# When ScalarE's Exps run and which engine copies attention's tiles out of PSUM

## The chip, the cores and the metric

The kernel runs on one core of one Trainium2 chip. The metric is the device time in microseconds (us) of one execution, the median over several runs. Five engines work side by side, each on its own list of instructions in a fixed order: TensorE (PE in the profile; PEld are its weight loads), VectorE (DVE), ScalarE (ACT), GpSimd (POOL) and SyncE (SP), which here issues DMAs. TensorE writes to PSUM; VectorE and ScalarE read from it.

## The reference

Attention through 32 inducing points over 4 batches of 12480 tokens of 128 values, and behind it, on all 49920 rows, a feed-forward part of 2048 hidden values with a rational function between its two matrices:

```python
def mab(q, kv):
    s = scale * (q @ kv.transpose(0, 2, 1))
    s = s - s.max(-1, keepdims=True)
    a = np.exp(s)
    a /= a.sum(-1, keepdims=True) + 1e-09
    return a @ kv
h = mab(I, x)          # 32 inducing points attend to all tokens of the batch
x = mab(x, h)          # each token attends to the 32 results
...
h = x @ w_in
P = a[0] + a[1] * h + a[2] * h2 + a[3] * h3          # h2 = h*h, h3 = h2*h
Q = 1.0 + np.abs(b[0]) * np.abs(h) + np.abs(b[1]) * h2
return (P / (Q + 1e-06)) @ w_out
```

## The kernel before

**The feed-forward part** sets the beat. The hidden values lie across the 128 partitions, in 16 chunks. A block is 480 tokens, and a unit of work is one block and one pair `q` of chunks, a tile of 128x960: 4 batches x 26 blocks x 8 pairs are 832 units. `fast_ticks` (L777) writes out one tick for each unit, in which the stages of several units are interleaved: `first` makes `hp` in PSUM (TensorE, from the attention weights `at` and a table `st` of the batch), VectorE takes `u` from `hp` and makes a product `l`, GpSimd makes another `l` from `u`, ScalarE works on `u`, and `second` sums `po` from `l` and `w_out`. In even ticks VectorE has `u<-hp` and `l<-u,all,hp`, and GpSimd `l<-u,all`; in odd ticks VectorE has `l<-l,all,u` and `l<-hp,all,l`, and GpSimd `u<-l,all` and `l<-u`. Once in a block, `fetch` (L762) copies `po` to `oT` on VectorE, and SyncE stores it.

**ScalarE** computes the quotient through Ln and Sigmoid, which need different function tables. So it works in turns of eight ticks: four Lns on two units each (`u<-u`, 128x1920), a table load, four Sigmoids on the same (`u<-u,all`), a table load, and between them four Abs of later units (`u<-hp,all`). There are 104 turns. An Exp needs a table of its own; the Exps of attention stand at the place `turn == 4`, behind the Abs that follows the last Ln and ahead of the first Sigmoid, so that a turn with Exps has three table loads instead of two.

**Attention** runs beside it as Python generators that `side` (L680) moves on once in each tick. Each `yield` names what the next step costs on VectorE ("v"), TensorE ("pe") or GpSimd ("g"), and `side` takes it if the tick's share (`SPARE`) covers it; in one tick a generator takes steps of one kind only. Two generators run:

- `attend` works on the tokens of the batch at hand (`pass3`, L545): scores `pd` on TensorE, `amx` and `a` on VectorE, Exp of `a` on ScalarE, then `quotients` (L591): sums `asm` on VectorE, the scaling of `a` on GpSimd, transposes `pa` on TensorE, a rounded copy `hl[.,0]` of `pa` and, by VectorE, what the rounding left, `hl[.,1]`. `spread` sends `hl` to the tiles `at` by DMA.
- `ahead` (L633) prepares the next batch: `pass1` (L334) writes the scores of all tokens to `e`, seven groups of 480 columns; `exp_rows` (L380) takes their Exp in place, two groups at a time; `pooled` (L403) transposes `e` to `pt`, copies that to `eT` and sums `ph` with `x` on TensorE. Then come the tables `st` of the batch (`piece`, `linear`).

Two places of this have queues. An Exp is put in `exp_q` by `flush` (L395), and `run_act` (L224) issues all that is there at the next `turn == 4`. A copy on ScalarE goes through `act` (L214): it is put in `act_q`, issued a tick later, and its generator moves on after that. PSUM has one tile (`misc`) for all of attention's results; a generator holds it from the first matmul to `free`.

In what follows, `boot` is the time before the first unit, in which the first batch is prepared with nothing beside it. All engine calls pass through one helper, so that nearly all rows of the profile have its line, L157, and tiles are told apart by name.

Of the kernel before, what the change touches and what calls it, by code (L numbers as in the profile page):

```python
# [13 lines left out]
AF = mybir.ActivationFunctionType  # L14
# [3 lines left out]
P = 128  # L18
TP = 120
# [3 lines left out]
BT = HB * TP  # L23
# [149 lines left out]
class Kernel:  # L173
# [50 lines left out]
    def run_act(self, exps=True):  # L224
        while self.act_q and self.act_q[0][0] < self.tick:
            _, do, done = self.act_q.pop(0)
            do()
            done.append(1)
        if exps:
            for do in self.exp_q:  # L230
                do()
            self.exp_q = []

# [100 lines left out]
    def pass1(self, b):  # L334

        nc, ap = self.nc, self.ap
        X = mybir.AxisListType.X
        e = ap.tile([P, self.NG, BT], F32, tag="e", name=f"e{b}")
        mxs = ap.tile([P, self.NG, 2], F32, tag="mxs", name=f"mxs{b}")
        nc.gpsimd.memset(mxs, -3.0e38)  # L340
        xs = self.wide_columns(b) if self.boot else self.cols.pop((b, "a"))
        for g in range(self.NG):
            nb = min(4, self.NB - 4 * g)
            yield from self.landed("a", b, g)
            for j in range(nb):
                yield "pe", 0.8
                if j == 0:
                    pc = self.misc(f"pc{b}_{g}")
                nc.tensor.matmul(pc[:, 0:BT], self.ind[:, M * (3 - j):M * (7 - j)], next(xs), start=(j == 0), stop=(j == nb - 1))
            rows = slice(0, M * nb)  # L350
            for i in range(2):
                yield "v", 0.36
                c = slice(BT // 2 * i, BT // 2 * (i + 1))
                nc.vector.tensor_scalar(out=e[rows, g, c], in0=pc[rows, c], scalar1=1.0, scalar2=None, op0=ALU.mult, op1=ALU.max, accum_out=mxs[rows, g, i:i + 1])
            self.free()
        self.xs[b] = [self.x_rows(b, n) for n in range(4)]
        yield "v", 0.1
        mx = ap.tile([P, 1], F32, tag="mx", name=f"mx{b}")
        nc.vector.tensor_reduce(out=mx, in_=mxs.rearrange("p g i -> p (g i)"), axis=X, op=ALU.max)
        yield "pe", 0.2  # L360
        pm = self.misc(f"pm{b}")
        nc.tensor.transpose(out=pm[0:1, 0:P], in_=mx, identity=self.ident)
        yield "v", 0.3
        mt = ap.tile([1, 1, M], F32, tag="mt", name=f"mt{b}")
        nc.vector.tensor_reduce(out=mt[:, 0], in_=pm[0:1, 0:P].rearrange("o (j m) -> o m j", m=M), axis=X, op=ALU.max)
        self.free()
        nm = ap.tile([1, 4, M], F32, tag="H", name=f"nm{b}")
        nc.vector.tensor_scalar(out=nm, in0=mt.broadcast_to((1, 4, M)), scalar1=-1.0 / math.sqrt(C), scalar2=None, op0=ALU.mult)
        yield "pe", 0.2
        pb = self.misc(f"pb{b}")  # L370
        nc.tensor.matmul(pb[:, 0:4], nm.rearrange("o j m -> o (j m)"), self.ones, start=True, stop=True)
        yield "v", 0.1
        nmc = ap.tile([P, 1], F32, tag="nmc", name=f"nmc{b}")
        nc.vector.tensor_copy(out=nmc, in_=pb[:, 0:1])
        self.free()
        self.e[b] = e
        self.exps.append(lambda: self.exp_rows(b, e, nmc))
        self.flush()

    def exp_rows(self, b, e, nmc):  # L380

        g = self.e_done.get(b, 0)
        n = min(2, self.NG - g)
        rows = slice(0, M * min(4, self.NB - 4 * (g + n - 1)))
        if n == 2 and rows.stop < P:
            n, rows = 1, slice(0, P)
        self.nc.scalar.activation(e[rows, g:g + n], e[rows, g:g + n], AF.Exp, bias=nmc[rows], scale=1.0 / math.sqrt(C))
        self.e_done[b] = g + n
        if g + n < self.NG:
            if self.boot:  # L390
                self.exp_rows(b, e, nmc)
            else:
                self.exps.append(lambda: self.exp_rows(b, e, nmc))

    def flush(self):  # L395

        exps, self.exps = self.exps, []
        if self.direct:
            for do in exps:
                do()  # L400
        self.exp_q += [] if self.direct else exps

    def pooled(self, b, own=None):  # L403

        nc, ap = self.nc, self.ap
        e = self.e[b]
        acc = ap.tile([M, C + 1], F32, tag="acc", name=f"acc{b}")
        xs = self.xs.pop(b)

        def turned(g):  # L410
            rows = slice(0, M * min(4, self.NB - 4 * g))
            for c in range(HB):
                yield "pe", 0.22
                if c == 0:
                    pt = self.misc(f"pt{b}_{g}").rearrange("p (c n) -> p c n", c=HB)
                nc.tensor.transpose(out=pt[0:TP, c, rows], in_=e[rows, g, TP * c:TP * c + TP], identity=self.ident[rows, rows])
            eT = ap.tile([TP, HB, P], F32, tag="eT", name=f"eT{b}_{g}", bufs=2)
            yield from self.act(lambda: nc.scalar.activation(eT[:, :, rows], pt[0:TP, :, rows], AF.Identity, bias=0.0, scale=1.0))
            eTs.append(eT)

        eTs, early = [], int(self.boot)
        while self.e_done.get(b, 0) < self.NG:
            self.flush()
            yield "wait", 0
        if early:
            yield from turned(0)
        for g in range(self.NG):
            nb = min(4, self.NB - 4 * g)
            if g + early < self.NG:
                yield from turned(g + early)  # L430
            eT = eTs.pop(0)
            self.free()
            yield from self.landed("x", b, g)
            for k in range(HB * nb):
                j, c = divmod(k, HB)
                yield "pe", 0.2
                if k == 0:
                    ph = self.misc(f"ph{b}_{g}")
                if c == 0 and 0 < 4 * g + j < self.NB - 3:
                    xs.append(self.x_rows(b, 4 * g + j + 3))  # L440
                nc.tensor.matmul(ph[0:M, 0:C + 1], eT[:, c, M * j:M * j + M], xs[4 * g + j][:, c, :], start=(k == 0), stop=(k == HB * nb - 1))
            yield "v", 0.2
            if g == 0:
                nc.vector.tensor_copy(out=acc, in_=ph[0:M, 0:C + 1])
            else:
                nc.vector.tensor_tensor(out=acc, in0=ph[0:M, 0:C + 1], in1=acc, op=ALU.add)
            self.free()
        yield "v", 0.2
        rs = ap.tile([M, 1], F32, tag="rs", name=f"rs{b}")
        nc.vector.tensor_scalar(out=rs, in0=acc[:, C:], scalar1=1e-9, scalar2=None, op0=ALU.add)  # L450
        nc.vector.reciprocal(out=rs, in_=rs)
        yield "v", 0.2
        H = ap.tile([M, C], F32, tag="H", name=f"H{b}")
        nc.vector.tensor_scalar(out=H, in0=acc[:, 0:C], scalar1=rs, scalar2=None, op0=ALU.mult)
        yield "pe", 0.3
        pt = self.misc(f"HT{b}")
        nc.tensor.matmul(pt[:, 0:4 * M], H, self.ident4.rearrange("p a m -> p (a m)"), start=True, stop=True)
        yield "v", 0.2
        while own is None and self.scored < b - 2:
            yield "wait", 0  # L460
        HT = own if own is not None else ap.tile([C, 4 * M], F32, tag="HT", name=f"HT{b}", bufs=2)
        nc.vector.tensor_copy(out=HT, in_=pt[:, 0:4 * M])
        self.free()
        self.HT[b] = HT
# [80 lines left out]
    def pass3(self, b, groups):  # L545


        nc, ap = self.nc, self.ap
        X = mybir.AxisListType.X
        for fours in groups:  # L550
# [30 lines left out]

            if fours[-1] == self.NG - 1:
                self.scored = b
            self.exps.append(exps)
            self.flush()
            while not done:
                yield "wait", 0
# [3 lines left out]
    def quotients(self, b, r, nb, a):  # L591
        nc, ap = self.nc, self.ap
        rows = slice(0, M * nb)
# [10 lines left out]
        for c in range(HB):  # L604
            yield "pe", 0.25
            if c == 0:
                pt = self.misc(f"pa{b}_{r}")
            nc.tensor.transpose(out=pt[rows, TP * c:TP * c + TP], in_=a[:, c].rearrange("p j m -> p (j m)"), identity=self.ident[0:TP, 0:TP])
        hl = ap.tile([P, 2, BT], F32R, tag="hl", name=f"hl{b}_{r}", bufs=2)
        yield from self.act(lambda: nc.scalar.activation(hl[rows, 0], pt[rows, 0:BT], AF.Identity, bias=0.0, scale=1.0))  # L610
        yield "v", 0.65
        nc.vector.tensor_tensor(out=hl[rows, 1], in0=pt[rows, 0:BT], in1=hl[rows, 0].bitcast(F32), op=ALU.subtract)
        self.free()
# [335 lines left out]
```

## Time and profile before

| | before |
|---|---|
| runs | 2593.33, 2593.37, 2596.55 us; median 2593.37 us |
| profiled execution | 2594.75 us; its span 2592.9 us |
| granted TensorE clock, mean | 0.966 |
| busy share of the span | PE 87%, ACT 87%, DVE 85%, POOL 78% |
| instructions | PE 7508, DVE 2318, ACT 1590, POOL 1420 |
| table loads on ScalarE | 234, 300.2 us together |

The share of the span in which an engine is busy tells how full it is, and the chain that ended last tells whom the others wait for. In rows of the timeline the number in brackets is the engine's idle time ahead of the row, with the engine and tile that ended it.

### The profile page before, as it was taken

Reading aid. Unit: us, or ns where it says so; the run is one execution under the profiler, and the core shown is the slowest. Engines: PE = TensorE matmul, PEld = TensorE weight load, DVE = VectorE, ACT = ScalarE, POOL = GpSimd, SP = SyncE. Lnnn points to the kernel's source line nnn. Section 1 sums busy time; section 2 is a strip of 40 time slices with the busy share of each in tenths; the row PEclk is TensorE's granted clock in tenths of the full one; section 3 lists DMA queues with packets and bytes.
Section 4 is the critical chain, followed back from the end, with each engine's and each line's share of the span. In section 5 each row is a group of like instructions: output and inputs, shape, how many; then the busy total and the mean of one; then the engine's idle time right before and its main releaser. Section 6 shows DMA issues by size and latency. Waiting matters only on the chain.

```text
span 2592.9 us, 24006 instructions
## 1 busy us (share of the span) xinstructions
PE 2249.2 (87%) x7508; PEld 1233.8 (48%) x7508; DVE 2210.1 (85%) x2318; ACT 2244.9 (87%) x1590; POOL 2011.4 (78%) x1420
## 2 busy tenths in 40 slices
PE   7798888999899789989988898888888888888887
PEld 4544444555454355544544465444435434434333
DVE  6578778899899889899898888988889888888886
ACT  1488889989889999888899998899999999999996
POOL 2267767888787788888687887887888887888887
PEclk9699989999999999999999999999999999999999
DMA  7222201211222012112321131011101001000000
GB/s 251 73 62 78 73 27 52 71 50 31 70 83 80 19 31 76 50 48 63 92 55 48 35 88 38 16 42 31 46 27 50 27 20 38 20 22 24 17 17 17
DMA packets 117357, 133.68 MB, mean 52 GB/s; under 512 B 13544, under 2 KB 115816, under 8 KB 117224
## 3 DMA queue, kind: packets, MB, share of 16 engines
q1 hardware_dynamic: 117224, 132.06, 17.6%
q8 instruction: 64, 1.05, 0.2%
q14 instruction: 69, 0.57, 0.1%
HBM read 80.89 MB, written 25.56 MB: 41 GB/s over the span
## 4 chain that ended last, share of the span: by engine, by line
DVE 32%; PE 22%; ACT 19%; POOL 18%; issue 6%; DMA 1%; SPq 1%; DVEq 0%; POOLq 0%; ACTq 0%
DVE l L157 21%; ACT u L157 13%; POOL l L157 13%; PE po L157 13%; DVE u L157 7%; ACT L157 4%; POOL u L157 4%; PE hp L157 3%; PE ph L157 2%; PE pd L157 2%; DVE oT L157 1%; POOL a L157 1%; SPq L157 1%; DVE asm L157 1%; DMA x<-x_t 1%
## 5 line engine op out<-in xcount | busy, mean ns | idle before, releaser
L157 PE MATMUL po<-l,w_out 128*128 128x480 f32 x3328 | 1545.8, 592 | 188.4 <-POOL l L157 183.6
L157 PEld LDWEIGHTS po<-l,w_out 128*128 128x128 f32 x3328 | 607.3, 194 | 773.0 <-issue 419.7
L157 POOL TENSOR_TENSOR l<-u 128x960 f32<-128x960 f32 x416 | 932.2, 2241 | 34.7
L157 ACT ACTIVATE u<-u 128x1920 f32<-128x1920 f32 x416 | 739.8, 1799 | 193.2 <-DVE l L157 143.0
L157 PE MATMUL hp<-at,st 128*128 128x480 f32 x1664 | 742.7, 529 | 98.3 <-DVE l L157 91.1
L157 ACT ACTIVATE u<-u,all 128x1920 f32<-128x1920 f32 x416 | 766.1, 1887 | 1.2
L157 POOL TENSOR_SCALAR u<-l,all 128x960 f32<-128x960 f32 x416 | 445.5, 1071 | 392.8 <-DVE l L157 363.4
L157 DVE SCALAR_TENSOR_TENSOR l<-l,all,u 128x960 f32<-128x960 f32 x416 | 597.8, 1437 | 105.7 <-ACT u L157 105.3
L157 DVE SCALAR_TENSOR_TENSOR l<-hp,all,l 128x960 f32<-128x960 f32 x416 | 503.5, 1210 | 121.8 <-POOL l L157 114.0
L157 POOL TENSOR_SCALAR l<-u,all 128x960 f32<-128x960 f32 x416 | 555.6, 1336 | 64.7 <-DVE u L157 63.7
L157 DVE TENSOR_SCALAR u<-hp 128x960 int32<-128x960 int32 x416 | 477.0, 1147 | 75.6 <-PE hp L157 74.3
L157 PEld LDWEIGHTS hp<-at,st 128*128 128x128 f32 x1664 | 312.6, 193 | 431.3 <-issue 325.3
L157 DVE SCALAR_TENSOR_TENSOR l<-u,all,hp 128x960 f32<-128x960 f32 x416 | 500.3, 1203 | 0.3 <-ACT u L157 0.3
L157 ACT ACTIVATE u<-hp,all 128x960 f32<-128x960 f32 x416 | 434.7, 1045 | 36.4 <-PE hp L157 36.3
L157 ACT ACT_TABLE_LOAD x234 | 300.2, 1283 | 4.9 <-PEq L942 0.7
L157 PE MATMUL ph<-x,eT 120*32 120x129 f32 x832 | 105.8, 280 | 9.0 <-DMA x<-x_t 6.3
L157 PEld LDWEIGHTS pd<-HT,xTb 128*120 128x120 f32 x832 | 103.3, 198 | 9.7 <-DMA xTb<-x_c 4.3
L157 PE MATMUL pd<-HT,xTb 128*120 128x32 f32 x832 | 100.5, 277 | 5.2 <-DMA xTb<-x_c 4.1
L157 PEld LDWEIGHTS ph<-x,eT 120*32 120x32 f32 x832 | 88.9, 112 | 28.0 <-issue 21.5
L157 DVE COPY oT<-po 128x480 f32<-128x480 f32 x104 | 67.3, 647 | 21.6 <-PE po L157 21.3
L157 PE MATMUL po<-at,st 128*128 128x480 f32 x104 | 80.7, 776 | 0.0
L157 PE MATMUL pc<-xTa,ind 128*128 128x480 f32 x156 | 72.2, 566 | 1.9 <-DMA xTa<-x_c 1.9
(84 smaller groups left out, 621.6 us busy)
## 6 DMA issues: line engine op xcount, KB each, us to landing
x<-x_t SPq DMA_DIRECT2D x104, 240.0 KB, 3.5
xTb<-x_c SPq DMA_DIRECT2D x104, 240.0 KB, 2.8
at<-hl SPq DMA_DIRECT2D x416, 60.0 KB, 2.0
out<-oT SPq DMA_DIRECT2D x104, 240.0 KB, 2.0
xTa<-x_c SPq DMA_DIRECT2D x78, 240.0 KB, 2.8
xTw<-x_c SPq DMA_DIRECT2D x5, 960.0 KB, 10.3
raw<-w_in SPq DMA_DIRECT2D x4, 480.0 KB, 14.2
raw<-w_out SPq DMA_DIRECT2D x5, 384.0 KB, 5.9
```

The costliest lines, as they stand in the source:

```text
L157: ins = call(*args, **kw)
```

## The change

Two things are changed.

The Exps: each entry of `exp_q` now has a mark and the tick at which it came. The Exps of the tokens are marked `True` (soon), those of the batch ahead `False`. At `turn == 4` the queue is issued if an entry in it is marked soon or has waited 20 ticks; then all of it goes. And `exp_rows` takes up to three groups at a time (128x1440) instead of two (128x960).

The copies: outside `boot`, the copies `eT<-pt` and `hl<-pa` are VectorE's, as steps of kind "v" with a cost of 0.65, and don't go through `act` with its tick of delay.

```diff
@@ run_act
-        if exps:
-            for do in self.exp_q:
+        if exps and any(soon or self.tick - since >= 20 for do, soon, since in self.exp_q):
+            for do, _, _ in self.exp_q:
                 do()
             self.exp_q = []
@@ pass1
-        self.exps.append(lambda: self.exp_rows(b, e, nmc))
+        self.exps.append((lambda: self.exp_rows(b, e, nmc), False))
@@ exp_rows
-        n = min(2, self.NG - g)
+        n = min(3, self.NG - g)
         rows = slice(0, M * min(4, self.NB - 4 * (g + n - 1)))
-        if n == 2 and rows.stop < P:
-            n, rows = 1, slice(0, P)
+        if n > 1 and rows.stop < P:
+            n, rows = n - 1, slice(0, P)
...
-                self.exps.append(lambda: self.exp_rows(b, e, nmc))
+                self.exps.append((lambda: self.exp_rows(b, e, nmc), False))
@@ flush
-        self.exp_q += [] if self.direct else exps
+        self.exp_q += [] if self.direct else [(do, soon, self.tick) for do, soon in exps]
@@ pooled
-            yield from self.act(lambda: nc.scalar.activation(eT[:, :, rows], pt[0:TP, :, rows], AF.Identity, bias=0.0, scale=1.0))
+            if self.boot:
+                nc.scalar.activation(eT[:, :, rows], pt[0:TP, :, rows], AF.Identity, bias=0.0, scale=1.0)
+            else:
+                yield "v", 0.65
+                nc.vector.tensor_copy(out=eT[:, :, rows], in_=pt[0:TP, :, rows])
@@ pass3
-            self.exps.append(exps)
+            self.exps.append((exps, True))
@@ quotients
-        yield from self.act(lambda: nc.scalar.activation(hl[rows, 0], pt[rows, 0:BT], AF.Identity, bias=0.0, scale=1.0))
+        if self.boot:
+            nc.scalar.activation(hl[rows, 0], pt[rows, 0:BT], AF.Identity, bias=0.0, scale=1.0)
+        else:
+            yield "v", 0.65
+            self.cast(nc.vector, hl[rows, 0], pt[rows, 0:BT])
         yield "v", 0.65
         nc.vector.tensor_tensor(out=hl[rows, 1], in0=pt[rows, 0:BT], in1=hl[rows, 0].bitcast(F32), op=ALU.subtract)
```

Since a step of attention that is taken in another tick moves all that follow it, the order of the instructions changes in many places. Three of them, in rows of the built order (line, operation, result<-sources, shape; in `u_8_0` the numbers are block and pair, the last number only tells tiles apart).

ScalarE, in the first batch, around an Exp of the second batch's scores `e`; before, the first of four, which has a table switch to itself:

```order
L157 ACTIVATE u_9_0_1930<-hp_9_1_1927,all 128x960
L157 ACT_TABLE_LOAD
L157 ACTIVATE e_891<-e_891,nmc_1850 128x960
L157 ACT_TABLE_LOAD
L157 ACTIVATE u_8_0_1812<-u_8_0_1812,all 128x1920
```

and with the change, the second of three:

```order
L157 ACTIVATE u_12_0_2293<-hp_12_1_2290,all 128x960
L157 ACT_TABLE_LOAD
L157 ACTIVATE e_890<-e_890,nmc_1874 128x1440
L157 ACTIVATE a_5_2068<-a_5_2068 120x512
L157 ACTIVATE a_5_2068<-a_5_2068 120x4x64
L157 ACT_TABLE_LOAD
L157 ACTIVATE u_11_0_2184<-u_11_0_2184,all 128x1920
```

It is wider by half and stands with the Exps of the tokens, `a_5`, between one pair of table loads. The first of the three stands a turn earlier between two table loads of its own.

ScalarE, at the end of the Lns of block 5; before, a copy of the tokens' weights to `hl_2` stands behind the Abs of block 6:

```order
L157 ACTIVATE u_5_6_1487<-u_5_6_1487 128x1920
L157 ACTIVATE u_6_0_1514<-hp_6_1_1511,all 128x960
L157 ACTIVATE hl_2_1526<-pa_2_1521 128x480
L157 ACT_TABLE_LOAD
L157 ACTIVATE u_5_0_1396<-u_5_0_1396,all 128x1920
```

and with the change:

```order
L157 ACTIVATE u_5_4_1454<-u_5_4_1454 128x1920
L157 ACTIVATE u_5_6_1484<-u_5_6_1484 128x1920
L157 ACTIVATE u_6_0_1512<-hp_6_1_1509,all 128x960
L157 ACT_TABLE_LOAD
L157 ACTIVATE u_5_0_1389<-u_5_0_1389,all 128x1920
```

The copy is gone from this place between the last Ln and the first Sigmoid.

VectorE, around the rounding's rest `hl_5`; before, it stands in a tick whose number leaves 1 on division by 8 (the products of blocks 11 and 12 around it tell the tick):

```order
L157 TENSOR_SCALAR u_12_0_2309<-hp_12_0_2295 128x960
L157 SCALAR_TENSOR_TENSOR l_11_7_2311<-u_11_6_2280,all,hp_11_7_2277 128x960
L157 SCALAR_TENSOR_TENSOR l_10_6_2168<-l_10_6_2168,all,u_10_6_2164 128x960
L157 SCALAR_TENSOR_TENSOR l_12_0_2313<-hp_12_0_2295,all,l_12_0_2313 128x960
L157 TENSOR_TENSOR hl_5_2292<-pa_5_2287,hl_5_2292 128x480
```

and with the change:

```order
L157 TENSOR_SCALAR u_12_6_2375<-hp_12_6_2360 128x960
L157 SCALAR_TENSOR_TENSOR l_12_5_2377<-u_12_4_2346,all,hp_12_5_2343 128x960
L157 SCALAR_TENSOR_TENSOR l_11_4_2239<-l_11_4_2239,all,u_11_4_2235 128x960
L157 SCALAR_TENSOR_TENSOR l_12_6_2379<-hp_12_6_2360,all,l_12_6_2379 128x960
L157 TENSOR_SCALAR hl_5_2387<-pa_5_2382 128x480
L157 TENSOR_TENSOR hl_5_2387<-pa_5_2382,hl_5_2387 128x480
L157 TENSOR_SCALAR u_13_0_2407<-hp_13_0_2390 128x960
```

There the copy and the rest stand one behind the other on VectorE, six ticks later, in a tick that leaves 7.

More of the change, by code (lines that the diff above doesn't have):

```diff
@@ L398, in flush @@
         if self.direct:
-            for do in exps:
+            for do, _ in exps:
                 do()
-        self.exp_q += [] if self.direct else exps
+        self.exp_q += [] if self.direct else [(do, soon, self.tick) for do, soon in exps]
     def pooled(self, b, own=None):
```

## The prediction

> **What bounds the kernel now.** I read the engines' busy time first, then the chain of waits, and then one quiet turn row by row. A turn is eight ticks, that is one block of 480 tokens; I count it from the start of its first Sigmoid to that of the next turn. "Slot 3" means the ticks of `fast_ticks` whose number leaves 3 on division by 8.
>
> ```profile
> PE 2249.2 (87%) x7508; PEld 1233.8 (48%) x7508; DVE 2210.1 (85%) x2318; ACT 2244.9 (87%) x1590; POOL 2011.4 (78%) x1420
> DVE 32%; PE 22%; ACT 19%; POOL 18%; issue 6%; DMA 1%; SPq 1%; DVEq 0%; POOLq 0%; ACTq 0%
> ```
>
> Three engines stand within two points of each other and the chain spends its time on four of them, so none alone sets the pace. The chain of waits over one quiet turn near the end, where attention has nothing left to do, shows what does (start, us, engine and tile):
>
> ```profile
> 2457.12 1.90 ACT u L157
> 2459.05 0.38 DVE l L157
> ...
> 2461.48 0.57 DVE oT L157
> ...
> 2466.07 1.08 POOL u L157
> 2467.22 4.20 POOL l L157 x2
> 2471.45 1.22 DVE l L157
> ...
> 2473.73 1.13 DVE l L157
> 2474.95 2.75 ACT u L157 x2
> 2477.72 1.28 ACT L157
> 2479.01 1.90 ACT u L157
> ```
>
> It is a closed loop of 2479.01 − 2457.12 = 21.89 us: first Sigmoid, VectorE's products (with the copy `oT`), GpSimd's part of two pairs, VectorE again, the last Ln and the Abs behind it (2.75), a table load (1.28), the next Sigmoid. The timeline of the same turn shows the slack of those who wait (in brackets the idle time before a row, and who ended it):
>
> ```profile
> 2459.05 1.31 DVE L157 SCALAR_TENSOR_TENSOR l<-l,all,u 128x960 f32<-128x960 f32 x1 [0.67 <-ACT u L157]
> 2471.45 1.22 DVE L157 SCALAR_TENSOR_TENSOR l<-hp,all,l 128x960 f32<-128x960 f32 x1 [0.97 <-POOL l L157]
> 2476.87 1.22 DVE L157 SCALAR_TENSOR_TENSOR l<-hp,all,l 128x960 f32<-128x960 f32 x1 [0.89 <-POOL l L157]
> 2474.95 1.80 ACT L157 ACTIVATE u<-u 128x1920 f32<-128x1920 f32 x1 [1.22 <-DVE l L157]
> ```
>
> From this I take three rules. ScalarE waits 1.22 us before its last Ln, so a ScalarE copy anywhere between the first Sigmoid and that wait is free, while one between the last Ln and the Sigmoid (table load and Exp included) lies on the loop. An extra VectorE instruction is exposed in slots 3, 4 and 7, where VectorE works through from the Sigmoid to the pair that GpSimd needs (3, 4) or to the one that the last Ln needs (7). It is half covered in slots 5 and 6, where VectorE waits 0.97 for GpSimd, and covered in slots 0, 1 and 2, behind the last Ln's input, where 0.89 + 0.67 = 1.56 us of waits stand ready to take it.
>
> A later turn with attention's work in it bears this out.
>
> ```profile
> 1986.23 3.68 ACT L157 ACTIVATE u<-u,all 128x1920 f32<-128x1920 f32 x2
> 2005.34 1.80 ACT L157 ACTIVATE u<-u 128x1920 f32<-128x1920 f32 x1 [2.51 <-DVE l L157]
> ...
> 2009.41 1.06 ACT L157 ACTIVATE a<-a 120x1024 f32<-120x1024 f32 x1
> 2010.49 1.28 ACT L157 ACT_TABLE_LOAD   x1
> 2011.78 1.90 ACT L157 ACTIVATE u<-u,all 128x1920 f32<-128x1920 f32 x1
> ```
> ```profile
> 1991.64 0.66 DVE L157 COPY oT<-po 128x480 f32<-128x480 f32 x1 [0.84 <-PE po L157]
> 1992.22 0.68 DVE L157 TENSOR_REDUCE amx<-pd 120x16 f32<-120x512 f32 x1
> ...
> 1997.26 0.68 DVE L157 TENSOR_TENSOR a<-pd,amx 120x512 f32<-120x512 f32 x1
> ...
> 2005.17 0.68 DVE L157 TENSOR_REDUCE amx<-pd 120x16 f32<-120x512 f32 x1
> ...
> 2008.49 0.68 DVE L157 TENSOR_TENSOR a<-pd,amx 120x512 f32<-120x512 f32 x1
> ...
> 2013.71 1.22 DVE L157 SCALAR_TENSOR_TENSOR l<-l,all,u 128x960 f32<-128x960 f32 x1 [2.36 <-ACT u L157]
> ```
>
> It takes 2011.78 − 1986.23 = 25.55, or 3.66 over the quiet 21.89. Of that, 1.06 + 1.28 = 2.34 are the Exp and its second table load; the rest, 1.3, is what two VectorE rows in slots 3 and 5 (0.68 each) cost, for the wait before the last Ln grew from 1.22 to 2.51. The two rows in slots 0 and 1 (2005.17, 2008.49) cost nothing: VectorE still waits 2.36 for the Sigmoid. So exposed time counts at 1.29/1.36 = 0.95. And an earlier turn with two ScalarE copies off the loop:
>
> ```profile
> 927.14 0.58 ACT L157 ACTIVATE eT<-pt 120x512 f32<-120x512 f32 x1
> ...
> 936.11 0.56 ACT L157 ACTIVATE hl<-pa 128x480 fp32r<-128x480 f32 x1
> 938.57 1.80 ACT L157 ACTIVATE u<-u 128x1920 f32<-128x1920 f32 x1 [0.21 <-DVE l L157]
> 942.64 3.69 ACT L157 ACTIVATE u<-u,all 128x1920 f32<-128x1920 f32 x2
> ```
>
> The copies shrank the wait to 0.21 and the turn, begun at 920.82, took 21.82: no more than a quiet one. Most of what the change takes from ScalarE was free there.
>
> **The change part by part.** Durations, from the groups of instructions kept apart by shape (count | busy us, mean ns):
>
> ```profile
> L157 ACT ACT_TABLE_LOAD x234 | 300.2, 1283 | 4.9 <-PEq L942 0.7
> L157 ACT ACTIVATE e<-e,nmc 128x960 f32<-128x960 f32 x12 | 12.9, 1094 | 30.7 <-DVE nmc L157 30.6
> L157 ACT ACTIVATE e<-e,nmc 64x480 f32<-64x480 f32 x4 | 2.8, 692 | 0.0
> L157 ACT ACTIVATE eT<-pt 120x512 f32<-120x512 f32 x24 | 13.9, 583 | 19.6 <-PE pt L157 19.6
> L157 ACT ACTIVATE hl<-pa 128x480 fp32r<-128x480 f32 x24 | 13.4, 560 | 6.8 <-PE pa L157 4.6 <-PE po L157 1.1 <-PE hp L157 0.9
> L157 DVE COPY oT<-po 128x480 f32<-128x480 f32 x104 | 67.3, 647 | 21.6 <-PE po L157 21.3
> L157 DVE TENSOR_TENSOR hl<-pa,hl 128x480 fp32r<-128x480 f32 x24 | 15.6, 649 | 1.8 <-ACT hl L157 1.8
> L157 DVE TENSOR_REDUCE asm<-a 120x16 f32<-120x512 f32 x24 | 16.2, 675 | 0.8 <-ACT a L157 0.8
> ```
>
> *ScalarE's part of the loop (term 1).* In the built order the table loads fall from 234 to 230, and all four are second switches between the last Ln and the first Sigmoid: 4 × 1.283 = −5.1. The Exps of `e` outside the start go from nine of 128x960 and three of 64x480 to six of 128x1440 and the same three. No 1440 row exists; the line through 692 at 480 and 1094 at 960 gives 1496, so 9 × 1.094 − 6 × 1.496 = 0.9 less (bounds 0 and −0.9, since the work on the elements stays and only the fixed part can go). Of the 48 ScalarE copies that go (21 `eT`, 27 `hl`), four stand on the loop before (two of each), with one gate copy whose place shifts off it: about 5 × 0.57 = −2.9. The others ran under the 1.22 us wait and give nothing. Sum: −8.9.
>
> The Trainium skill ("ScalarE: Activation LUTs", section "What ACT_TABLE_LOAD costs") puts a switch at about 1283 ns of load and 1380 ns of drain. The load agrees with the row; the drain doesn't show, as the load at 2477.72 starts 0.02 behind the Abs and the Sigmoid follows it at once. By that page four switches would be worth 10.6 instead of 5.1.
>
> *VectorE (terms 2 and 3).* It gains those 48 instructions, each beside the 0.65 for a PSUM source of 480 columns (`oT`, `hl`) or 0.68 for 120x512 (`asm`'s row for its width); an `eT` of the last, half-filled group has fewer columns, about 0.41, scaled by width. In all 18 × 0.68 + 3 × 0.41 + 27 × 0.65 = +31. What of it counts hangs on the slots, and these move for all of attention's work, as the copies no longer wait for ScalarE and so shift what follows. I sorted all extras by slot from the built order, and priced them by the rows above and their like:
> - exposed (3, 4, 7): 87 → 123 instructions, 45.4 → 62.4 us (+17.0). Twelve `eT` and four `hl` copies come in, and the sums `asm` go from 8 to 17 and the gate scalings `gs` from 4 to 12, while the products `st` go from 8 to 3. Slot 7 alone gains 16.
> - half covered (5, 6): 75 → 92 instructions, 37.8 → 51.0 us, with 14 `hl` pairs in slot 6. Beyond 0.97 in each turn: 5.1 → 8.6 (+3.5).
> - covered (0, 1, 2): 132 → 127 instructions, 69.3 → 70.2 us. Beyond 1.56 plus the turn's Exp stretch it falls from 6.6 to 2.1; the straight lines below give this class no price, so I count nothing, and −4.5 as the bound.
>
> The price per exposed us I take as 1.0. A straight line through all turns of this trace, their length against the extras of each class, gave 0.9 to 1.3 for it, 0.1 to 0.5 for the half-covered, and about nothing for the covered ones. The lower bound is 0.5: before 1991.64 VectorE waits 0.84 for TensorE inside an exposed slot, and over the kernel 21.3 us go there ahead of `oT`, in which extras could vanish.
>
> *What else moves.* Nothing is queued behind a waiting Exp on ScalarE, as a closure held back issues nothing; what waits for it is `pooled` and then the next batch's tables, of which the built order still writes the last 512 columns in block 22 of 26 and the linear part in block 25, for use at the end of the block after next. On VectorE each new copy has the next pair's `u` behind it and waits itself for TensorE's transposes, issued at least a tick (2.7 us) earlier: 0. DMAs are the same in number. TensorE's attention matmuls bunch a little more (the most crowded turns have 8.4 us of them, from 7.8): 0, at worst +4. At the start the copies stay, and its Exps join: within 0.5 either way.
>
> **Sum:** −8.9 + 17.0 + 3.5 = +11.6 on the profiled execution's 2594.75 (span 2592.9 and 1.85 around it) gives 2606.4. The median of the runs is 1.4 below that execution, so I say **2605.0**. By the skill's page it would be +6.1. Ends: −8.9 − 4.5 + 0.5 × 17 = −5; −8.0 + 1.3 × 17 + 0.45 × 13.2 + 4 = +24.
>
> **The rivals.** (a) *All VectorE time is exposed.* If slots 5 and 6, filled with pairs, use up the wait for GpSimd and so delay the next pair, 31 of VectorE count: +22, 2615. For it: two copies in one tick make 1.3 us against 0.97. Against: the rows at 2005.17 and 2008.49. 0.11.
> (b) *Cancels.* Exposed extras fill TensorE's 21.3 us ahead of `oT` and count half: −8.9 + 8.5 + 1.8 = +1, 2595. 0.20.
> (c) *Faster.* VectorE's chain is not lengthened, since where the extra stands the wait for GpSimd or TensorE moves with it, and term 1 stays alone: −8.9, 2584.5. For it: every single VectorE wait quoted is of about the size of one copy. Against: 1.22 → 2.51 above. 0.20.
> (d) *ScalarE sets the pace.* Then all it sheds counts: 5.1 + 0.9 + 48 × 0.56 = 33, 2560. For it: 87%. Against: 1.22 us of idle time in every quiet turn, and 21.82 with two copies in it. 0.04. The Trainium skill ("Perfetto Trace Analysis", section "Identifying the Most-Contended Engine") would look at the fullest engine first, and that speaks for this one; the turn of 21.82 us speaks against it.
> That Exps don't join is none: the built order shows 26 → 22 Exp stretches.
>
> **How the numbers follow.** My forecast has 0.45, the rivals 0.11, 0.20, 0.20 and 0.04. A measurement of this kernel tells 0.2% (5 us) from no change. Slower: 0.45 + 0.11 = 0.56; same: 0.20; faster: 0.24. The likeliest case's own range is 2598 to 2611; 8 in 10 needs (b) and (c) and half of (a): 2584 to 2618. Left out are (d), the lower half of (c) and the upper of (a), some 0.2.
>
> **What would show it.** Right: 230 table loads; VectorE's busy time up by about 31, ScalarE's down by about 33; the wait for VectorE ahead of ScalarE's Lns (143.0 us in the row below) larger by 25 to 45, since ScalarE loses work inside that wait and the loop grows; quiet turns still 21.9; turns with slot-7 extras longer by their rows' length. Wrong: if turns with extras in slots 3, 4 and 7 stay at 21.9, or if `hl` pairs in slot 6 lengthen their turn by more than 1.3 − 0.97.
>
> ```profile
> L157 ACT ACTIVATE u<-u 128x1920 f32<-128x1920 f32 x416 | 739.8, 1799 | 193.2 <-DVE l L157 143.0 <-POOL l L157 46.9 <-POOL x L157 2.2
> ```

## The result: slower, and by more than twice what was forecast

| | before | with the change |
|---|---|---|
| median of the runs (lowest, highest) | 2593.35 us (2590.50, 2596.55) | 2621.82 us (2620.76, 2629.04) |
| ratio to before | | 1.0115 (95% interval 1.0094 to 1.0137) |
| span of the profiled execution | 2592.9 | 2619.3 |
| turns 0 to 101 together, over 21.9 us each | 189.1 | 221.4 |
| of it turns 0 to 5 | 28.5 | 35.2 |
| of it turns 22 to 29, 48 to 55 and 74 to 81 (around the switches to the next batch) | 36.8 | 65.0 |
| of it all others | 123.7 | 121.2 |

Forecast were +11.6 us and at most 2618; measured are +28.5. The lower part of the table is summed over the lengths of the turns, from first Sigmoid to first Sigmoid; the turns are counted from 0, and 26 of them make a batch. Outside the start of the kernel and the three switches of batches the change even wins 2.5 us. Where the time is lost doesn't yet tell why, since the change also moves work from one turn to another. (The time ahead of the first Sigmoid, 121.8 us before and 115.7 after, tells nothing: in two kernels of the runs below whose instructions are the same up to there, the probes in slots 5 and 1, it was 115.9 and 121.2.)

The page after, busy times and the engines' shares of the chain:

```profile
PE 2252.6 (86%) x7508; PEld 1229.1 (47%) x7508; DVE 2232.2 (85%) x2366; ACT 2217.3 (85%) x1534; POOL 2006.3 (77%) x1420
DVE 32%; PE 25%; ACT 17%; POOL 14%; issue 5%; DMA 2%; SPq 2%; DVEq 0%; ACTq 0%; POOLq 0%
```

ScalarE is 28 us less busy and VectorE 22 us more; in the chain TensorE (22% to 25%), the DMAs and SyncE's queue have grown. The groups of instructions by shape show the sizes of the change itself:

```profile
L157 ACT ACT_TABLE_LOAD x230 | 295.1, 1283 | 4.8 <-PEq L950 0.7
L157 ACT ACTIVATE e<-e,nmc 128x1440 f32<-128x1440 f32 x8 | 11.9, 1494 | 30.4 <-DVE nmc L157 30.3
L157 DVE TENSOR_SCALAR hl<-pa 128x480 fp32r<-128x480 f32 x23 | 14.9, 649 | 0.6 <-issue 0.4
L157 DVE COPY eT<-pt 120x512 f32<-120x512 f32 x18 | 12.3, 681 | 0.0
L157 DVE COPY eT<-pt 120x256 f32<-120x256 f32 x3 | 1.2, 413 | 0.0
```

All are as estimated, to 3 ns: 1494 for the wide Exp, 649 and 681 for the copies. The lines that no part of the prediction spoke of are among the waits (engine and tile, released by whom: us, times, longest), before and then after:

```profile
PEld pd L157 <- DMA xTb<-x_c: 4.3, 2, 2.5
PE pd L157 <- DMA xTb<-x_c: 4.1, 2, 2.4
```
```profile
PEld pd L157 <- DMA xTb<-x_c: 14.1, 8, 2.5
PE pd L157 <- DMA xTb<-x_c: 13.2, 8, 2.4
```

TensorE waits for the loads of the tokens' columns, three times as long. Three turns show where: number 23, 49 and 75, each the 24th of its batch, take 31.71, 32.04 and 31.81 us; before, these took 23.27, 22.15 and 21.89. The chain of waits through turn 75 (1950.14 to 1981.95):

```profile
1946.26 2.99 DMA xTb<-x_c
1949.25 0.04 issue
1949.29 1.02 PE pd L157 x8
...
1957.61 0.57 DVE oT L157
1958.19 0.02 issue
1958.20 0.34 SPq L157
1958.55 0.05 issue
1958.59 0.03 SPq L157
1958.62 0.03 issue
1958.65 2.91 DMA xTb<-x_c
1961.56 0.04 issue
1961.61 1.02 PE pd L157 x8
1962.63 5.00 PE po L157 x8
```

Two loads stand in the chain, and ahead of the second one SyncE: its store of `oT` had to wait for VectorE's copy, and the load was the next in the queue. What SyncE did there, in its own timeline:

```profile
1940.25 5.96 SPq L157 DMA_DIRECT2D at<-hl  x8
1946.26 2.02 SPq L157 DMA_DIRECT2D xTb<-x_c  x4
1958.20 0.34 SPq L157 DMA_DIRECT2D out<-oT  x1
1958.65 1.82 SPq L157 DMA_DIRECT2D xTb<-x_c  x4
```

Ahead of the first load stand eight small DMAs `at<-hl`, which keep SyncE's queue for 5.96 us.

### The profile page after: what moved, and what is told of

Same layout as the page of the kernel before. It is cut to its first block, busy times and chain, and to the rows that moved or that the text cites. A ratio compares the mean times of both kernels' runs of the same rounds, so it can differ in the third digit from the quotient of the medians.

```text
span 2619.3 us, 23913 instructions
## 1 busy us (share of the span) xinstructions
PE 2252.6 (86%) x7508; PEld 1229.1 (47%) x7508; DVE 2232.2 (85%) x2366; ACT 2217.3 (85%) x1534; POOL 2006.3 (77%) x1420
## 4 chain that ended last, share of the span: by engine, by line
DVE 32%; PE 25%; ACT 17%; POOL 14%; issue 5%; DMA 2%; SPq 2%; DVEq 0%; ACTq 0%; POOLq 0%
DVE l L157 20%; PE po L157 14%; ACT u L157 13%; POOL l L157 11%; DVE u L157 7%; ACT L157 4%; PE hp L157 4%; PE ph L157 3%; POOL u L157 3%; SPq L157 2%; PE pd L157 2%; DVE oT L157 1%; DVE asm L157 1%; DMA xTb<-x_c 1%; PE pc L157 1%
## 5 line engine op out<-in xcount | busy, mean ns | idle before, releaser
L157 DVE SCALAR_TENSOR_TENSOR l<-l,all,u 128x960 f32<-128x960 f32 x416 | 584.4, 1405 | 104.2 <-ACT u L157 104.2
L157 DVE SCALAR_TENSOR_TENSOR l<-hp,all,l 128x960 f32<-128x960 f32 x416 | 503.5, 1210 | 115.9 <-POOL l L157 106.9
L157 ACT ACT_TABLE_LOAD x230 | 295.1, 1283 | 4.8 <-PEq L950 0.7
```

Source lines behind the costliest of these rows:

```text
L157: ins = call(*args, **kw)
```

## The experiments

Theory A was that these late loads are what the prediction missed; B, that the copies cost VectorE more than I took; C, that the Exps' wait makes the next batch's preparation late, so that work piles up at the switch.

### Loads written out earlier

`columns` issues the load of a group's fourth block only when the first block of that group is asked for. The first kernel writes each load out right behind the last score matmul of the block whose buffer it takes:

```diff
@@ columns
                 if n + 4 < self.NB:
                     ts.append(self.x_columns(b, n + 4, kind))
+                if kind == "b":
+                    yield
@@ pass3
                     nc.tensor.matmul(pc[0:TP, M * j:M * j + M], xT[...], self.HT[b][:, 0:M], start=True, stop=True)
+                    if j % HB == HB - 1:
+                        next(self.cols[b, "b"])
```

> The changed kernel, but each load of the tokens' columns xTb is written out right behind the last score matmul of the block whose buffer it takes, instead of when the next block is asked for; nothing else is edited. Theory A (late loads: in turns 23, 49 and 75 TensorE waits twice for the load of a group's fourth block, which SyncE has only just issued; each such turn is 6.9 us longer than the VectorE slots and table loads account for, 20.8 together): the three turns fall from 31.8 to about 25, TensorE's wait for xTb from 13.2 to under 3, the time from 2621.8 to 2601 (to 2610 if TensorE's crowd of matmuls stays in the way). Theory B (the copies on VectorE cost more per us than I took) and theory C (the Exps' wait moves the next batch's tables to the batch's end, where two generators' work collides): within 5 us of 2621.8.

Measured: 2599.32 us, ratio to before 1.0026 (1.0015 to 1.0036); TensorE no longer waits for `xTb`, and turns 23, 49 and 75 take about 26.75 us each. 22.5 us came back, as A has it; B and C don't allow for that. The control on the kernel before:

> The kernel before with the earlier xTb loads alone, a control for the first run. TensorE waits 4.1 us for xTb before, so there is little to win; the order of attention's work moves a little (excess by slots and table loads 131.2 against 125.2): 2590 to 2600 by every theory. Much faster than 2590 would mean that the loads cost more than their waits show.

Measured: 2611.37 us, 1.0066 (1.0052 to 1.0080), slower and outside all expectations. The edit also moves attention's ticks, since `landed` now sees the loads: by the names of the tiles, 1981 of the 7508 places in TensorE's order hold another matmul than without the edit, against 134 in the changed kernel. Here other loads (`xTa`, 6.6 us of TensorE's waits from 1.9) became late as well, and the control doesn't tell what the edit itself is worth. So loads had to be made punctual without moving anything else; that is the third set of runs.

### Each part alone

The Exps' part with the copies left on ScalarE, and the copies' part with the Exps as before:

> Only the Exps' part of the change: the queue waits and takes three groups, the copies eT and hl stay on ScalarE with their delay. The next batch's HT then comes in block 22, 21 and 21 of the batch, against 18, 14 and 10 before and 20, 20 and 20 with the whole change. Theory A or B: table loads and slots give 127.9 us of excess over quiet turns, against 125.2 before, so 2593 to 2598. Theory C: 2605 to 2618, with long turns near the end of each batch.

> Only the copies' part of the change: eT and hl by VectorE without a delay, the Exps two groups at a time and at the next switch. VectorE's slots by the built order: exposed 54.3 us (before 45.4, whole change 62.4), half covered 60.6 (37.8, 51.0), covered 68.8. Excess over quiet turns by the prices of the prediction 134.4 us against 125.2: 2602. Theory B: 2612 or more. Theory C: 2602 or less, since the next batch's HT comes in blocks 18, 13 and 6, early.

Measured: 2653.77 us, 1.0241 (1.0227 to 1.0255), and 2644.87 us, 1.0206 (1.0192 to 1.0220). Both parts alone are slower than both together, which none of the theories had: the Exps' part lies above every expectation for it, the copies' part where only B (2612 or more) put it. The chain through turn 50 of the Exps' part (35.47 us long) shows SyncE's queue at its worst: from the store of `oT` on, the chain runs for over 10 us through it and sixteen DMAs `at<-hl`, and then a load lands and TensorE goes on:

```profile
1357.44 0.33 SPq L157
...
1358.48 0.54 SPq L157
...
1359.07 0.58 SPq L157
...
1367.52 0.59 SPq L157
...
1368.15 2.96 DMA xTb<-x_c
...
1371.15 1.81 PE pd L157 x8
```

Each small DMA takes SyncE about 0.59 us, so two tiles `at` (sixteen of them) ahead of a load delay it by some 10 us. Which loads are hit depends on where the ticks fall; that this is why the two parts' costs don't add is tested next.

### SyncE's queue alone

Here `at<-hl` and `out<-oT` are put in a list and written out a tick later, two in a tick, while loads are written out at once. Every instruction on TensorE, VectorE, ScalarE and GpSimd keeps its place, in all four kernels by the names of the tiles in their traces; only SyncE's order differs.

```diff
@@ spread
-                    self.nc.sync.dma_start(out=at[M * k:M * k + M, j].bitcast(F32), in_=hl[rows, k % 2].bitcast(F32))
+                    self.later_dma(1, at[M * k:M * k + M, j].bitcast(F32), hl[rows, k % 2].bitcast(F32), (b, 2 * r + h))
@@ fetch
-        self.nc.sync.dma_start(out=self.out[:, t:t + BT], in_=oT)
+        self.later_dma(1, self.out[:, t:t + BT], oT)
@@ side
         self.tick += 1
+        self.run_dma(2)
...
+    def run_dma(self, most):
+        while self.dma_q and most and self.dma_q[0][0] <= self.tick:
+            _, out, in_, _ = self.dma_q.pop(0)
+            self.nc.sync.dma_start(out=out, in_=in_)
+            most -= 1
```

The list is emptied ahead of a first use of `at` and of a new `hl`.

> The kernel before with SyncE's queue alone changed: the small DMAs of spread (at<-hl, eight for a tile) and the store out<-oT are held back by a tick and written out two in a tick, while loads go at once; on TensorE, VectorE and ScalarE every instruction stands in the order of before. Theory D (loads of attention that stand in SyncE's queue behind eight at<-hl at 0.6 us each, or behind a store that waits for oT, come late, and TensorE's fixed order turns that into a stall of everything): TensorE's waits for loads, 12 us before, fall by half or more, 2575 to 2588. Theory E (what the order costs beyond VectorE's slots is TensorE's own crowd of attention matmuls): 2590 to 2596, no change.

> The changed kernel with the same change of SyncE's queue alone; the order on TensorE, VectorE and ScalarE is the changed kernel's. Theory D: from 2621.8 to 2595 or less, since its 31 us beyond slots and table loads are mostly late loads, and what stays over the run above is the slots' share, 134.3 - 125.2 = 9 us. Theory E: 2615 to 2622.

> The Exps' part alone with the same change of SyncE's queue. Theory D: from 2653.8 to 2600 or less; over the kernel before with this queue about 3 us by slots and table loads (127.9 against 125.2). Theory E: above 2640.

> The copies' part alone with the same change of SyncE's queue. Theory D: from 2644.9 to 2605 or less; over the kernel before with this queue about 9 us by slots and table loads (134.4 against 125.2). Theory E: above 2630.

| | queue as it was | queue relieved | ratio to before as it was |
|---|---|---|---|
| before | 2593.0 | 2579.12 | 0.9960 (0.9946 to 0.9975) |
| whole change | 2621.82 | 2596.71 | 1.0017 (1.0007 to 1.0028) |
| Exps' part | 2653.77 | 2608.98 | 1.0057 (1.0041 to 1.0074) |
| copies' part | 2644.87 | 2599.68 | 1.0033 (1.0021 to 1.0045) |

All four fall, by 14, 25, 45 and 45 us, and TensorE's waits for `xTb` are gone, but for one of 1.3 us in the Exps' part. That the queue costs this much (D) is shown, and that TensorE's crowd alone accounts for the excess (E) falls. In size D holds for before and the copies' part; the whole change and the Exps' part stay above the 2595 and 2600 that it had at most. Also, the edit relieves loads of the small DMAs and of the stores that wait for VectorE at once, and what each of the two is worth wasn't separated. The whole change, turn 75, takes 25.94 us instead of 31.81, with these rows at the place (TensorE, chain of waits):

```profile
1932.95 2.21 PE pd L157 x21
1935.16 0.51 PE hp L157 x2
1935.67 0.97 PE pd L157 x10
1936.64 3.30 PE po L157 x8
```

The score matmuls go on without a load between them. Of the 28.5 us that the change costs, 28.5 − 17.6 = 10.9 are thus the queue's, that is late loads that it has beyond those of before. 17.6 stay, where D's text had 9; the Exps' part keeps 30, where it had 3.

### What a VectorE instruction costs in each slot

On before with the relieved queue, one more VectorE instruction in each turn, whose result nobody uses:

```diff
@@ fast_ticks
+            if t % 8 == 7 and 16 <= t < n:
+                V.tensor_reduce(out=self.probe, in_=self.w_in[:, 0:512], axis=mybir.AxisListType.X, op=ALU.max)
             self.side(u or units[-1])
```

> The kernel before with the relieved SyncE queue (2579.1 us), and in every turn but the first two one more VectorE instruction in slot 7, a maximum over 128x512 of w_in that nobody uses (about 0.68 us by asm's row, 102 of them, 69 us of VectorE). All other instructions keep their order. By the prediction's slots it is exposed at a price of 1.0: 2648 (2641 to 2669 for 0.9 to 1.3). Rival, VectorE's share of the span decides wherever the work stands: slots 7, 5 and 1 cost the same.

> The same with the instruction in slot 5. By the prediction's slots it is half covered: free in a turn with nothing else in slots 5 and 6, exposed beyond 0.97 us otherwise, +19.7 by the built order: 2599. Rival as for slot 7.

> The same with the instruction in slot 1. By the prediction's slots it is covered up to 1.56 us in a turn: at most +9.5, 2579 to 2589. Rival as for slot 7.

Measured: 2618.03, 2596.06 and 2600.27 us, that is 39, 17 and 21 over the 2579.12 without it. (The kernel before, measured again with each set of runs, had medians of 2592.5 to 2595.6, so a difference between sets is good to about 3 us.) Slot 5 came out 3 us under the expected 2599; slot 7 cost less than the 62 us at least that were expected, and slot 1 more than the 10 at most. The group in the first of them:

```profile
L157 DVE TENSOR_REDUCE probe<-w_in 128x1 f32<-128x512 f32 x102 | 68.7, 674 | 0.0
```

In the quiet turns the slots do what the prediction said. A quiet turn took 21.88 without a probe, 22.41 with slot 7, 22.10 with slot 5 and 21.88 with slot 1. The wait ahead of the last Ln, in the timeline of ScalarE, for slots 7, 5 and 1 in this order:

```profile
2470.88 1.80 ACT L157 ACTIVATE u<-u 128x1920 f32<-128x1920 f32 x1 [1.73 <-DVE l L157]
```
```profile
2471.10 1.80 ACT L157 ACTIVATE u<-u 128x1920 f32<-128x1920 f32 x1 [1.44 <-DVE l L157]
```
```profile
2458.80 1.80 ACT L157 ACTIVATE u<-u 128x1920 f32<-128x1920 f32 x1 [1.22 <-DVE l L157]
```

From 1.22 it grows by 0.51, 0.22 and 0. So an exposed us of row costs 0.52/0.674 = 0.77, not 1.0. A part of that is that rows of VectorE overlap:

```profile
2490.34 0.68 DVE L157 TENSOR_REDUCE probe<-w_in 128x1 f32<-128x512 f32 x1
2490.94 1.15 DVE L157 TENSOR_SCALAR u<-hp 128x960 int32<-128x960 int32 x1
```

A row of 0.68 has its successor 0.60 later. In turns with attention's work the rules blur: outside the 24 turns that are quiet without a probe, slot 7 costs 23.8 us together, slot 5 10.7 and slot 1 18.9, though it cost nothing in the quiet ones. It is neither the rival (all slots alike) nor the prediction whole.

### TensorE's crowd

What stays beyond slots might be attention's matmuls standing together in a tick. The share of TensorE that `side` may give out in one tick is capped:

```diff
-    SPARE = {"v": (0.36, 1.45, 1.45), "g": (0.9, 2.5, 2.5), "pe": (0.75, 2.5, 1.7)}
+    SPARE = {"v": (0.36, 1.45, 1.45), "g": (0.9, 2.5, 2.5), "pe": (0.75, 1.5, 1.0)}
```

> The kernel before with the relieved SyncE queue, and TensorE's share for attention in one tick capped at 1.0 us instead of 1.7 (kept over 1.5 instead of 2.5), so that sixteen matmuls ph or twenty-two pd no longer stand in one tick. The order moves: exposed VectorE time 36.6 us (45.4), half covered 47.9 (37.8), excess by slots and table loads 117.6 us (125.2). If only slots and table loads count: 2571.5. If TensorE's crowd is the rest of the excess (51 us beyond slots in the kernel before with this queue): 2545 to 2566.

> The kernel before with TensorE's cap alone, SyncE's queue as it was. If queue and crowd add up: 2593 less 26 for the cap, 2567. If late loads take the cap's gain away (the loads' order and the ticks move): 2575 to 2600.

> The changed kernel with the relieved SyncE queue and TensorE's share for attention capped at 1.0 us in a tick, as in the last run of before. The order moves: exposed VectorE 55.2 us, excess by slots and table loads 138.0, against 117.6 for before with the same two edits (2553.0). If late loads and TensorE's crowd were all that the prediction left out, the slots' 20.4 us stay (13 to 16 at the price of 0.77 that the probe in slot 7 showed): 2566 to 2574, and TensorE's share of the chain, 28% with the queue alone, falls to about 20%. If the copies cost in another way: above 2580.

> The Exps' part alone with the same two edits. With the queue alone it is 30 us over before, of which slots and table loads explain 3. If TensorE's crowd is the rest: 2550 to 2565, near before with the two edits (2553.0). If the rest is the late tables of the next batch (HT in block 22 or later): above 2570.

> The copies' part alone with the same two edits. With the queue alone it is 20 us over before, of which slots explain 9. If TensorE's crowd is the rest: 2555 to 2566. If VectorE's copies cost more than their slots: above 2570.

| | queue relieved | queue relieved and cap | ratio to before as it was |
|---|---|---|---|
| before | 2579.12 | 2553.00 | 0.9835 (0.9817 to 0.9854) |
| whole change | 2596.71 | 2618.44 | 1.0096 (1.0081 to 1.0112) |
| Exps' part | 2608.98 | 2604.90 | 1.0039 (1.0025 to 1.0054) |
| copies' part | 2599.68 | 2591.55 | 0.9989 (0.9980 to 0.9997) |

The kernel before wins 26 us by the cap, and 20 by it alone (2573.47; 0.9919, 0.9904 to 0.9933; TensorE then waits 9.9 for `xTb`). The order moves too, and by the expectation's count 7.6 of the 26 are slots and table loads; the rest fits a crowd, but wasn't taken apart further. With both it is 1.6% faster than before and beats every other version. Its page:

```profile
PE 2233.1 (88%) x7508; PEld 1211.7 (47%) x7508; DVE 2205.8 (86%) x2318; ACT 2243.1 (88%) x1589; POOL 2023.8 (79%) x1420
DVE 35%; POOL 21%; PE 20%; ACT 17%; issue 5%; DMA 1%; DVEq 0%; POOLq 0%; SPq 0%; ACTq 0%
```

But in the three variants of the change the cap doesn't bring back the rest: the whole change becomes slower by it, against its expectation, and neither part comes near 2553. The turns show that two things happen at once. Outside the switches of batches the cap wins 11.4 us in the whole change and 28.9 in the Exps' part, as it wins 25.1 in before. At the switches the two lose: the excess there goes from 46.2 to 83.4 in the whole change (turn 24 alone takes 36.65 us, with the steps of the next batch's tables in its chain) and from 76.2 to 99.6 in the Exps' part, while before has 35.9 and 38.3. That fits a crowd as a cost in these two as well, and capped ticks that are too small for a preparation that is late; neither was tested alone. In the copies' part with the cap, ScalarE waits for VectorE for 189.6 us ahead of its Lns; in before with the cap for 147.1. There the copies' part (48 copies, 31 us of rows) costs 38.5 us over before, more than all the copies' own time, where the theory of the crowd had at most 13. And in the turns around the switches of batches, the excess of the Exps' part is 99.6 us against 38.3 of before, while in the others, from turn 6 on, it is below it (80.2 against 92.4). This points to C, which the next expectations call L, as does the 2604.90, which the expectation for late tables had (above 2570).

### The Exps' wait and the wider Exps

With queue and cap as in the best version, of the Exps' part only the wider Exps (`>= 0` in place of `>= 20` ticks), and only the wait (two groups at a time):

```diff
-        if exps and any(soon or self.tick - since >= 20 for do, soon, since in self.exp_q):
+        if exps and any(soon or self.tick - since >= 0 for do, soon, since in self.exp_q):
```
```diff
-        n = min(3, self.NG - g)
+        n = min(2, self.NG - g)
```

> Before with the relieved SyncE queue and TensorE's cap (2553.0), and of the Exps' part the wider Exps alone: three groups at a time, issued at the next switch without a wait. HT of the next batch comes in blocks 19, 18 and 16 of the batch, as early as without it; slots and table loads 125.8 us against 117.6, and 123.7 for the Exps' part with its wait (2604.9). Theory L (the Exps' wait makes the next batch's preparation late, so that it piles up before the switch of batches and TensorE and the tiles at fall behind): 2553 to 2563. Theory S (slots and table loads decide): 2559 to 2606, near the kernel with the wait.

> The same with the wait alone: two groups at a time, held for up to 20 ticks or the tokens' Exps. The four Exps of a batch stand three turns apart and HT comes only in the last block of each batch. Slots and table loads 137.6 us against 117.6. Theory L: 2620 or more, with the long turns in the last two blocks of a batch and the first ones of the next, and waits of TensorE for at. Theory S: 2568 to 2575.

Measured: 2570.47 us, 0.9906 (0.9884 to 0.9927), and 2687.77 us, 1.0353 (1.0326 to 1.0380). With the wait alone, turns 24, 50 and 76 take 68.8 us each. Inside the first (691.73 to 760.5) the chain holds nothing but attention from 706.10 to 752.93:

```profile
706.10 2.57 PE ph L157 x22
...
711.96 0.29 DVE acc L157
...
713.83 1.31 PE pg L157 x2
...
719.37 6.59 PE pd L157 x32
```

The next batch's tables were not ready when the first block of it was due, and `until` writes out all the missing steps at one place, during which the other work stands still. Of the 52 us that the Exps' part costs over 2553.00, 34 go without the wait (2570.47), so the wait is most of it. The width alone is still 17 over 2553.00, where up to 10 were expected; the slots account for 8 of it. The run with the wait alone shows the mechanism but not its size in the change, since with two groups at a time the tables come later still: by the expectations in the last block of each batch, against blocks 22, 21 and 21 in the Exps' part and 20 in the whole change.

## Why the prediction was wrong

*Direction, and why.* Slower was right, and was given 0.56. It isn't luck alone, for with SyncE's queue relieved in both kernels the change still costs 17.6 us. But the time lies outside the range, and what put it there, the 10.9 us of late loads, stands in no term of the sum. With them taken out, 17.6 against +11.6 is inside the range. Where the loss stands wasn't seen either: the +11.6 were a sum over all turns, and outside start and switches the change was worth −2.5 us.

*ScalarE's part of the loop (term 1).* Its sizes hold: 230 table loads of 1283 ns, the wide Exp 1494 for 1496 estimated. That ScalarE's other copies were free rests on the turn of 21.82 us with two of them; that ScalarE lost 28 us of work (33 were forecast) and the kernel gained nothing agrees with it, but doesn't show it. The Trainium skill ("ScalarE: Activation LUTs", section "What ACT_TABLE_LOAD costs") has a switch at 2.66 us with its drain; no run here changes table loads alone, so this stays open beyond the 1283 ns of the row.

*VectorE (terms 2 and 3).* The copies' rows sum to 31, as said; VectorE's busy time rose by 22, since rows of other work shortened, above all these (597.8 before):

```profile
L157 DVE SCALAR_TENSOR_TENSOR l<-l,all,u 128x960 f32<-128x960 f32 x416 | 584.4, 1405 | 104.2 <-ACT u L157 104.2
```

The three classes of slots are borne out in quiet turns by the probes, with a price of 0.77 for slot 7, 0.33 (0.22/0.674) for slot 5 and 0 for slot 1. The prediction's 0.95 was misread: of the two rows in the turn of 25.55 us, one stands in slot 5, which the prediction itself calls half covered, yet both were counted whole. At the probes' prices they make 0.75 of the 1.29 us (an estimate, with slot 3 at the price of slot 7), and VectorE waited 0.84 for TensorE in the same turn. In turns with attention's work slot 1 wasn't free. And with the crowd capped, the copies' part costs 38.5, so the sum over slots doesn't carry over to such a kernel. Whether that is VectorE's time as such, as rival (a) has it, or the moved order of attention stays open; 38.5 is more than (a) has for the copies (31).

*What else moves: the step that failed.* The prediction said "DMAs are the same in number" and counted nothing for them. Equal in number they are; their places in SyncE's queue are not. The copies without a delay and the Exps' wait shift attention's ticks so that loads come to stand behind eight `at<-hl` or behind a store that waits for `oT`. TensorE takes its work in a fixed order, so a load that is 2 us late stops the whole loop: turn 75, with two such waits, takes 31.81 us, and 25.94 without them. The queue alone brings back 25.1 us in the changed kernel and 13 to 14 in before: 10.9 of the difference. The start is wholly of this kind, with 26.6 us in both kernels once the queue is relieved. I had read the chain's "SPq 1%" as nothing. The prediction's only margin here, "0, at worst +4", stood for TensorE's bunched matmuls. Another zero, that a new copy waits for nothing but TensorE's transposes, is off by little: two of them wait 1.2 us together for DMAs `at<-hl`.

*"the linear part in block 25, for use at the end of the block after next".* I took the later tables for early enough. The run with the wait alone shows the mechanism by which they may not be (68.8 us turns). For the whole change itself it isn't shown: with the relieved queue its longest turn from turn 20 on takes 27.5 us, and the chain of turn 75 shows score matmuls and the sum `po` there, not steps of the tables. Of the 17.6 us that stay, 10.3 lie in the switches of batches (46.2 against 35.9) and 5.7 in the other turns, but a part of that may be only work that stands in another turn than before. How much of the 17.6 is the Exps' wait, how much the copies and how much the crowd wasn't separated, since each part alone moves the ticks of the other; that cause stays open.

*What would show it.* 230 table loads and quiet turns of 21.88 us came as said. The wait of ScalarE for VectorE ahead of the Lns was to grow by 25 to 45 us; it grew by 11.5:

```profile
L157 ACT ACTIVATE u<-u 128x1920 f32<-128x1920 f32 x416 | 738.2, 1798 | 237.3 <-DVE l L157 154.5 <-POOL l L157 81.7
```

The wait for GpSimd's `l` grew by 34.8 instead (46.9 before). The late loads didn't make it, for with the relieved queue it is still 73.5 us, against 36.8 in before with that queue. Whether VectorE's extra rows reach ScalarE by way of GpSimd, or attention's own rows on GpSimd do it, no run here separates; the sign looked at one of two waits. The other signs: a row in slot 7 lengthens a quiet turn by 0.52 us of its 0.674. Pairs `hl` in slot 6 were to lengthen a turn by no more than 1.3 − 0.97 = 0.33; turns 84 and 88 with one take 22.01 and 22.11, and turn 92 takes 22.86, where the copy waited 0.83 for a DMA. Of the rivals, (b) and (c) are out, also by the 17.6 us that stay without the late loads, and (d), ScalarE as the pace, is refuted by its 28 us less work.

## What to carry to other kernels

When a change moves work between ticks, look at every queue that feeds an in-order engine, and ask of each load what stands ahead of it there and since when; an unchanged number of DMAs says nothing. Compare parts of a change only after such a chance effect is taken out (here by changing SyncE's order alone); even then parts that move each other's order needn't add up, as here, where with the relieved queue they cost 30 and 21 us alone and 18 together. Work that is put off to save a switch has a due time somewhere: find the step that needs it and how far away it is.

## What was not expected of the hardware

The small DMAs of 60 KB took SyncE about 0.59 us each to issue (the loads and stores of 240 KB 0.34 in the median), so that eight cost 5 to 6 us of its queue, more than the 2.9 us that a load of 240 KB takes to land. The Trainium skill ("DMA: Bandwidth & Descriptors", section "Issuing engines are not separate DMA queues") says that issuing from several engines saves only the time on the sequencer, "which is usually small relative to the DMA itself". Here it was not small: this time, together with stores that wait for VectorE in the same queue, was worth 14 to 45 us in four kernels, where both stood ahead of loads that TensorE needed.
